# Part of the attention scores of later batches computed in early slots and kept in DRAM

## The chip, the cores and the metric

The kernel runs on one core of a Trainium2 chip. The metric is the time of one execution on the device, in microseconds (us); the median of three runs counts. Five engines work side by side: TensorE (PE in the profile, with its weight loads as PEld), VectorE (DVE), ScalarE (ACT), GpSimd (POOL) and SyncE (SP), which here mainly sends DMA transfers.

## The reference

Two blocks follow each other. The first is attention in which every query keeps only its 32 largest scores; the second sends every token to one of eight experts.

```python
# attention: batch 8, heads 8, sequence 576, head width 64
scores = scale * np.matmul(q, k.transpose(0, 1, 3, 2))
kth = np.partition(scores, -top_k, axis=-1)[..., -top_k:-top_k + 1]      # top_k = 32
scores = np.where(scores >= kth, scores, -1000000000.0)
scores = scores - np.max(scores, axis=-1, keepdims=True)
attn = np.exp(scores)
attn = attn / (np.sum(attn, axis=-1, keepdims=True) + 1e-09)
x = np.matmul(attn, v)          # then (B,H,S,D) -> (4608, 512)

# experts: 8 of them, 512 -> 1024 -> 512
logits = x @ w_gate
expert_idx = np.argmax(logits, axis=1)
...                             # gate_w: softmax value of the chosen expert
for e in range(E):              # over the rows sorted by expert
    h = np.maximum(x_sorted[lo:hi] @ w1[e], 0.0)
    y_sorted[lo:hi] = h @ w2[e]
out = gate_w[:, None] * y
```

All values are float32.

## The kernel before

The attention is cut into units of two heads (U = 4 units in each of B = 8 batches), and each unit into tiles of 128 queries. A slot of the main loop handles a pair of tiles, so there are 18 slots in a batch and 144 in all. The slots of a batch run in this order: four for the first unit, one for the remaining 64 queries of the first and second unit, four for the second unit, and the same for the third and fourth unit.

```python
def products(tiles):                              # TensorE: the scores
    ...
        ps = k.ps_s.tile([P, 2, SM], F32, name="sc")
    ...
    for half in range(2):
        for n, ps, h, rows, cols, first in todo:  # alternates between the two heads
            ...
            nc.tensor.matmul(ps[rows, j, 0:HF], n.q[d, cols], n.k[d, keys], start=True, stop=True)

def scores(got):                                  # ScalarE: PSUM to SBUF
    s = k.att.tile([P, 2, 2, HF], F32, name="s", bufs=2 if k.exact else 4)
    return s, [
        lambda m=m, ps=ps: nc.scalar.copy(s[:, m, :, :], ps[:, :, 0:HF]) for m, ps in enumerate(got)
    ]

def fold(s):                                      # VectorE: larger and smaller halves
    f.h = k.att.tile([P, 2, HF], F32, name="h", bufs=1)
    nc.vector.tensor_tensor(f.h, s[:, :, 0, :], s[:, :, 1, :], op=ALU.max)
    f.l = k.att.tile([P, 2, HF], F32, name="l")
    nc.vector.tensor_tensor(f.l, s[:, :, 0, :], s[:, :, 1, :], op=ALU.min)
```

The search for the 32nd largest score runs on VectorE (`MAX8` and `MATCH_REPLACE8`, four rounds). Then ScalarE computes `low` and a steep ramp, GpSimd subtracts it (`less`), ScalarE takes the exponential, and TensorE transposes the weights and multiplies them with the values. Small VectorE steps, such as the reciprocal of the row sums, wait in a list `aside` and are put one at a time between the instructions of a search (`tick`).

The main loop, cut to what matters here. The engines TensorE, ScalarE and VectorE get their instructions in the order of this text; SyncE and GpSimd are ordered by the scheduler of the framework.

```python
AHEAD = 3
for i, (b, g) in enumerate(work):
    ...
    if i + 1 < len(work):
        f_of[i + 1] = fold(s_of[i + 1])
        then = lambda: fold_on(f_of[i + 1])
    low, nbias, doubts = search(tiles, s_of[i], f_of.pop(i), then)
    at_place("small")
    w_of[i] = depths(s_of[i], low)                # ScalarE
    less(s_of.pop(i), w_of[i])                    # GpSimd
    ...
    if i + AHEAD < len(work):
        s_of[i + AHEAD], steps = scores(got_of.pop(i + AHEAD))
        for step in steps:
            step()
    evacuate()
    at_place("turn")
    turns = turning(i - 1) if i else iter(())
    next(turns, None)                             # transposes, copies
    part = min(BETWEEN, now - now // 2)
    rest = pieces(part)                           # pieces of expert blocks (TensorE)
    next(turns, None)
    rest = pieces(now - now // 2 - part + rest)
    weights(tiles, w_of[i], nbias)                # ScalarE: exponentials
    next(turns, None)
    evacuate()
    if i + AHEAD + 1 < len(work):
        multiply(i + AHEAD + 1)                   # products four slots ahead
    ...
```

The expert blocks (128 rows each) start in the third batch, when the rows of complete blocks are known. A block needs its rows from DRAM and the two weights of its expert, all sent by SyncE; two pairs of weight buffers exist. How many pieces a slot takes follows from a rate fixed in the program.

```python
def load_weights(n, expert):
    e = nc.sync.value_load(expert, min_val=0, max_val=E - 1)
    n.w1 = k.wp.tile([P, 1, DT, F], F32, name="w1")
    nc.sync.dma_start(n.w1, w1v[:, bass.ds(e, 1), :, :])      # 2 MiB
    n.w2 = k.wp.tile([P, 1, FT, Dm], F32, name="w2")
    nc.sync.dma_start(n.w2, w2v[:, bass.ds(e, 1), :, :])      # 2 MiB
    return n
```

Of the kernel before, what the change touches and what calls it, by code (L numbers as in the profile page):

```python
# [9 lines left out]
F32 = mybir.dt.float32  # L10
# [25 lines left out]
def kernel(  # L36
# [6 lines left out]
    moe_w2: bass.AP,  # L43
    out: bass.AP,
):

# [34 lines left out]
    nc = tc.nc  # L83
    B, U, P, _ = qk.shape
    N, Dm = out.shape
    S = N // B
    E = moe_w_gate.shape[1]
    F = moe_w1.shape[2]
    D = P // 2
    NC = 4  # L90
    SM = NC * P
    ST = S - SM
    KC = NC + 1
    HF = S // 2
# [4 lines left out]
    DT = Dm // P  # L99
    FT = F // P  # L100
# [18 lines left out]
    k = SimpleNamespace()  # L119
# [48 lines left out]
    for odd in range(2):  # L168
        for h in range(2):
            r = slice(h * D, (h + 1) * D)  # L170
            at = odd * (lw + P) + h * E
# [107 lines left out]
    def scores(got):  # L279
# [5 lines that stand above are left out]
# [445 lines left out]
    ON_CHIP = 3  # L730
    KEEP = 3 * PIECES
    BETWEEN = 2

    with fast:
        units = [(b, u) for b in range(B) for u in range(U)]
# [67 lines left out]
        def ending(b, u):  # L803

            nonlocal left
            n = unit[b * U + u]
            if u == 0:
                x_of[b] = k.xp.tile([P, KC, XW], F32, name="x")
                in_turn(token_ids(x_of[b][:, :, Dm + 1].bitcast(I32), b))
                lg_of[b] = k.small.tile([P, KC, E], F32, name="lg")  # L810
            x, lg = x_of[b], lg_of[b]
            out_steps = outputs(n, x)
            yield "products"
            next(out_steps)
            yield "relu"
            next(out_steps)
            if u % 2 == 0:
                yield "relu"
            div = divisors(n)
            next(div)  # L820
            aside.append(div)
            yield "products"
            next(out_steps)
            if b * U + u + 2 < len(units):
                load_values(unit[b * U + u + 2])
            yield "relu"
            next(out_steps)
            yield "products"
            next(out_steps)
            yield "relu"  # L830
            next(out_steps, None)
            yield "rows"
            through(div)
            logits(n, lg)
            rows(n, x)
            if u < U - 1:
                return
            yield "small"
            r = choice(lg)
            aside.append(r.steps)  # L840
            yield "weights"
            yield "turn"
            through(r.steps)
            nc.scalar.activation(lg, lg, AF.Exp)
            yield "products"
            ranks(r)
            yield "small"
            steps = places(r, x)
            aside.append(steps)
            yield "relu"  # L850
            nc.scalar.copy(run, r.run)
            yield "pool"
            through(steps)
            scatters.extend(scattering(r, x))
            if b == B - 1:
                scatter(KC)
                slot_i = k.small.tile([1, 2, NSLOT], I32, name="slot_i")
                through(table(slot_i, SURE, False))
                firsts = [(slot_i[0:1, 0, j:j + 1], slot_i[0:1, 1, j:j + 1]) for j in range(SURE)]
                ready = load_rows(SimpleNamespace(), firsts[0][1], True)  # L860
            new = LAST - SURE if b == B - 1 else new_of[b]
            if new:
                slot_i = slot_last if b == B - 1 else k.small.tile([1, 2, NSLOT], I32, name="slot_i")
                steps = table(slot_i, new, b == B - 1)
                aside.append(steps)
                yield "weights"
                yield "pool"
                yield "weights"
                yield "pool"
                through(steps)  # L870
                coming.extend((slot_i[0:1, 0, j:j + 1], slot_i[0:1, 1, j:j + 1]) for j in range(new))
            if b == B - 1:
                spare.extend(coming[ALWAYS - SURE:])
                del coming[ALWAYS - SURE:]
                assert len(loaded) == 2 and not waiting
                fill_up()
                coming[0:0] = [(firsts[0][0], ready)] + [(expert, (piece,)) for expert, piece in firsts[1:]]
                scatter(0)
# [9 lines left out]

        got_of, s_of, f_of, w_of = {}, {}, {}, {}

        def tiles_of(i):
            b, g = work[i]
            return [(unit[b * U + u], tile) for u, tile in g]
# [3 lines left out]

        def multiply(i):
            tiles = tiles_of(i)
            got_of[i] = products(tiles)  # L900
            n, tile = tiles[0]
            more = n.b * U + n.u + 2
            if tile == (NC - 1 if n.u % 2 else 2 * NC) and more < len(units):
                unit.append(load_unit(*units[more]))

        def loop():
            nonlocal credit, rate, clock
            for i in range(min(AHEAD, len(work))):
                multiply(i)
                s_of[i], steps = scores(got_of.pop(i))  # L910
                for step in steps:
                    step()
            multiply(AHEAD)
            f_of[0] = fold(s_of[0])
            fold_on(f_of[0])
            for i, (b, g) in enumerate(work):
                tiles = tiles_of(i)
                u, tile = g[0]
                if tile == 0 and u % 2 == 0:
                    open_unit(tiles[0][0])  # L920
                if tails(tiles):
                    open_unit(tiles[1][0])

                then = lambda: None
# [5 lines that stand above are left out]
                w_of[i] = depths(s_of[i], low)  # L930
                less(s_of.pop(i), w_of[i])
                doubts()
                put_stores()
                scatter(1)
                at_place("pool")
                at_place("relu")
                at_place("rows")
                at = i % per_batch
                if at == FIRST and b:
                    rate = new_of[b - 1] * PIECES / (U * NT)  # L940
                credit += rate * len(g)
                room = left
                if b == B - 1 and at >= ARRIVED:
                    room -= KEEP
                    credit = room / (len(work) - i)
                share = {0: 0.5, 1: 1.2, 2: 1.6, 3: 0.5, 2 * NC: 1.4}[tile]
                now = max(0, min(int(credit * share + 0.5), room))
                credit -= now
                clock = i
                if i + AHEAD < len(work):  # L950
                    s_of[i + AHEAD], steps = scores(got_of.pop(i + AHEAD))
                    for step in steps:
                        step()
                evacuate()
                at_place("turn")
                turns = turning(i - 1) if i else iter(())
                next(turns, None)
                part = min(BETWEEN, now - now // 2)
                rest = pieces(part)
                next(turns, None)  # L960
                rest = pieces(now - now // 2 - part + rest)
                weights(tiles, w_of[i], nbias)
# [3 lines that stand above are left out]
                    multiply(i + AHEAD + 1)  # L966
                if tile == NC - 1:
                    end = ending(b, u)
                    late.append([end, next(end)])
                at_place("products")  # L970
                at_place("weights")
                credit = min(credit + pieces(now // 2 + rest), 6 * rate)

            for _ in turning(len(work) - 1):
                pass
            assert len(late) == 1
            clock = None
            for place in late[0][0]:
                if place == "rows":
                    pieces(4)  # L980
            kept = left - ALWAYS * PIECES
            assert kept >= 0, kept
            k.apart = True
            pieces(kept)
# [135 lines left out]
```

## Time and profile before

| | |
|---|---|
| median of 3 runs | 1374.13 us (1373.11 to 1375.44) |
| span of the profiled execution | 1370.3 us |
| PE busy | 1234.6 us (90%) |
| DVE busy | 1084.5 us (79%) |
| ACT busy | 932.0 us (68%) |
| POOL busy | 661.5 us (48%) |
| DMA | 231.68 MB, mean 169 GB/s |

The shares are means over stages that differ. A view that cuts the span into stretches shows the busy time of each engine in each of them. A view of the waits says for which instruction of which engine another one stood idle, how long in total, how often, and how long at most. A tile's view lists the instructions that read or write it, with the shortest, median and longest duration in ns. A timeline lists instructions by start and duration in us; `x8` means that eight were merged. `SPq` is SyncE's queue: the time at which it sends a transfer. L290 is line 290 of the kernel.

### The profile page before, as it was taken

Reading aid. Unit: us, or ns where it says so; the run is one execution under the profiler, and the core shown is the slowest. Engines: PE = TensorE matmul, PEld = TensorE weight load, DVE = VectorE, ACT = ScalarE, POOL = GpSimd, SP = SyncE. Lnnn points to the kernel's source line nnn. Section 1 sums busy time; section 2 is a strip of 40 time slices with the busy share of each in tenths; the row PEclk is TensorE's granted clock in tenths of the full one; section 3 lists DMA queues with packets and bytes.
Section 4 is the critical chain, followed back from the end, with each engine's and each line's share of the span. In section 5 each row is a group of like instructions: output and inputs, shape, how many; then the busy total and the mean of one; then the engine's idle time right before and its main releaser. Section 6 shows DMA issues by size and latency. Waiting matters only on the chain. (4 is left out here: it accounts for less than half of the span.)

```text
span 1370.3 us, 24487 instructions
## 1 busy us (share of the span) xinstructions
PE 1234.6 (90%) x7666; PEld 838.6 (61%) x7666; DVE 1084.5 (79%) x4591; ACT 932.0 (68%) x2113; POOL 661.5 (48%) x805
## 2 busy tenths in 40 slices
PE   5777677687799999999999999999999999999995
PEld 3444444344466666766666666767676677776773
DVE  8999999999999999999999999999999820000000
ACT  4788877877888888888877788887777821111110
POOL 3455557555654666566556665565557621000000
PEclk8788787877999999999999999999999999999998
DMA  2100011001583267427654474357542859999880
GB/s 82 29 29 29 28 36 56 29 29 44 178 296 124 89 232 266 142 72 261 226 174 168 166 274 148 113 188 293 184 167 75 308 183 358 390 325 331 301 321 18
DMA packets 102220, 231.68 MB, mean 169 GB/s; under 512 B 5182, under 2 KB 25918, under 8 KB 102080
## 3 DMA queue, kind: packets, MB, share of 16 engines
q1 hardware_dynamic: 95328, 209.76, 43.8%
q0 software_dynamic: 6464, 19.97, 4.0%
q8 instruction: 62, 1.02, 0.3%
q14 instruction: 78, 0.64, 0.1%
q10 hardware_dynamic: 288, 0.30, 0.1%
HBM read 208.72 MB, written 22.33 MB: 169 GB/s over the span
## 5 line engine op out<-in xcount | busy, mean ns | idle before, releaser
L379 POOL TENSOR_TENSOR w<-s,w 128x576 f32<-128x576 f32 x288 | 409.5, 1442 | 432.3 <-ACT w L370 432.3
L687 PE MATMUL ph<-xTs,w 128*128 128x128 f32 x2560 | 308.6, 276 | 6.0 <-ACT xTs L664 6.0
L687 PEld LDWEIGHTS ph<-xTs,w 128*128 128x128 f32 x2560 | 297.4, 192 | 26.4 <-issue 19.1
L702 PE MATMUL py<-w,hT 128*128 128x512 f32 x640 | 292.2, 596 | 0.0
L338 DVE MAX8 tops<-scr 128x8 f32<-128x168 f32 x864 | 245.5, 316 | 0.0
L276 PE MATMUL sc<-qkb 64*128 64x288 f32 (+1 forms) x1280 | 221.6, 472 | 9.5 <-ACT s L283 5.2
L387 ACT ACTIVATE w<-w,nbias 128x576 f32<-128x576 f32 x288 | 224.0, 792 | 3.5 <-POOL w L379 2.5
L370 ACT ACTIVATE w<-s,low 128x576 f32<-128x576 f32 x288 | 207.6, 768 | 4.7
L398 PE MATMUL wTm<-turn,w 128*128 128x128 f32 x1152 | 171.2, 289 | 29.0 <-ACT xl L450 17.7
L398 PEld LDWEIGHTS wTm<-turn,w 128*128 128x128 f32 x1152 | 133.1, 146 | 89.6 <-issue 35.4
L999 DVE CAST any_i<-pd 1x1 int32<-1x1 f32 x1 | 0.1, 146 | 236.0 <-PE pd L997 236.0
L702 PEld LDWEIGHTS py<-w,hT 128*128 128x128 f32 x640 | 114.4, 190 | 117.6 <-issue 116.5
L345 DVE MATCH_REPLACE8 scr<-tops,scr 128x168 f32<-128x168 f32 x576 | 176.9, 311 | 0.0
L283 ACT COPY s<-sc 128x576 f32<-128x576 f32 x288 | 169.1, 641 | 10.5 <-PE sc L276 10.5
L404 ACT COPY wT<-wTm 128x512 f32<-128x512 f32 x256 | 139.1, 604 | 38.9 <-PE wTm L398 38.6
L276 PEld LDWEIGHTS sc<-qkb 64*128 64x128 f32 (+1 forms) x1280 | 118.2, 195 | 72.9 <-issue 26.6
L432 PE MATMUL po<-wT,vb 128*64 128x288 f32 x1024 | 157.8, 457 | 0.4 <-ACT wTt L419 0.4
L708 POOL DMA_INDIRECT out_dram<-y,xg x40 | 43.1, 1078 | 211.9 <-ACT y L716 199.8
L329 DVE MAX8 few<-l 128x8 f32<-128x288 f32 x288 | 127.2, 442 | 0.0
L432 PEld LDWEIGHTS po<-wT,vb 128*64 128x64 f32 x1024 | 75.3, 152 | 78.0 <-issue 29.3
L692 ACT ACTIVATE hT<-ph 128x512 f32<-128x512 f32 x80 | 48.6, 608 | 107.3 <-PE ph L687 107.3
L290 DVE TENSOR_TENSOR h<-s 128x576 f32<-128x576 f32 x144 | 117.0, 812 | 5.8 <-ACT s L283 5.8
(116 smaller groups left out, 1433.4 us busy)
## 6 DMA issues: line engine op xcount, KB each, us to landing
w<-in_moe_w_dram SPq DMA_DIRECT2D x80, 2048.0 KB, 9.6
qkb<-in_qk_dram SPq DMA_DIRECT2D x31, 608.0 KB, 4.3
xg<-x_rows SPq DMA_DIRECT2D x40, 257.0 KB, 10.0
vb<-in_v_dram SPq DMA_DIRECT2D x32, 320.0 KB, 3.2
x_rows<-blank SPq DMA_DIRECT2D x5, 257.0 KB, 14.7
x_rows<-blank POOLq DMA_DIRECT2D x4, 257.0 KB, 8.5
x_rows<-x,posi POOLq DMA_INDIRECT x40, 3.1
out_dram<-y,xg POOLq DMA_INDIRECT x40, 6.1
```

The source lines that it names most:

```text
L276: nc.tensor.matmul(ps[rows, j, 0:HF], n.q[d, cols], n.k[d, keys], start=True, stop=True)
L283: lambda m=m, ps=ps: nc.scalar.copy(s[:, m, :, :], ps[:, :, 0:HF]) for m, ps in enumerate(got)
L338: nc.vector.max(out=tops[:, m, r * 8:(r + 1) * 8], in_=src[m])
L345: nc.vector.match_replace(out=scr[:, m, :], in_to_replace=tops[:, m, r * 8:(r + 1) * 8], in_values=src[m], imm_value=NEG,)
L370: nc.scalar.activation(w[:, m, :], s[:, m, :, :].rearrange("p j k -> p (j k)"), AF.Relu, scale=-STEEP, bias=low[:, m:m + 1],)
L379: k.last_pool = in_turn(nc.gpsimd.tensor_tensor(w[:, m, :], s[:, m, :, :].rearrange("p j k -> p (j k)"), w[:, m, :], op=ALU.subtract)).ins
L387: nc.scalar.activation(w[:, m, :], w[:, m, :], AF.Exp, scale=scale, bias=nbias[:, m:m + 1], accum_out=n.z[:, c:c + 1])
L398: nc.tensor.transpose(pm[:, c * P:(c + 1) * P], w[:, m, first:first + P], ident)
L404: nc.scalar.copy(wT[:, :, m, q], pm4)
L432: nc.tensor.matmul(po[r, 0:HF], n.v[:, c, r], rhs, start=(c == 0), stop=(c == KC - 1))
L687: nc.tensor.matmul(ph[:, f, :], n.w1[:, 0, dt, fc * P:(fc + 1) * P], n.xT[:, dt, :], start=(dt == 0), stop=(dt == DT - 1),)
L702: nc.tensor.matmul(py, hT[:, f, :], n.w2[:, 0, f, :], start=(f == 0), stop=(f == FT - 1))
```

## The change

For the fifth, sixth and seventh batch, the scores of the fourth unit's eight full tiles (four slots of a batch, twelve in all) are no longer computed in those batches. Every second slot from the second on computes half of such a pair of tiles instead, copies it to the SBUF and, when both halves are there, stores it in DRAM. The space for the unit's queries and keys and for two pairs of finished scores is taken from weight buffers, which aren't used yet at that time. Where the scores are wanted, a transfer brings them from DRAM into the buffer `s`, in the place where ScalarE copied them from PSUM. It is meant to take work from TensorE and ScalarE in a stage in which both are full, and to do it in a stage in which they are not. Besides, the reciprocal of the row sums is put on the list `aside` later.

```diff
+    EARLY_FOR = (4, 5, 6)
...
             div = divisors(n)
             next(div)
-            aside.append(div)
             yield "products"
             next(out_steps)
             ...
             yield "relu"
             next(out_steps)
+            aside.append(div)
             yield "products"
...
+        early = {}
+        for i, (b, g) in enumerate(work):
+            if b in EARLY_FOR and g[0][0] == U - 1 and g[0][1] < NC:
+                early[i] = dram.tile([P, 2, 2, HF], F32, name=f"early{i}")
+
+        def earlier():
+            todo = sorted(early)
+            own = []
+            def open_own(p):
+                ...                                # room: a buffer of w1 (p even) or w2
+                nc.sync.dma_start(room[:, 0:2 * S + ST], qk[work[todo[p * NC]][0], U - 1, :, :])
+                own.append(room)
+            open_own(0)
+            for at, i in enumerate(todo):
+                if at % NC == 0:
+                    open_own(at // NC + 1)
+                ...
+                for m in range(2):
+                    ps = k.ps_s.tile([P, 2, SM], F32, name="sc")
+                    d = slice(m * D, (m + 1) * D)
+                    for j in range(2):
+                        keys = ...
+                        nc.tensor.matmul(ps[:, j, 0:HF], room[d, cols], room[d, keys], start=True, stop=True)
+                    nc.scalar.copy(put[:, m, :, :], ps[:, :, 0:HF])
+                    if m:
+                        nc.sync.dma_start(early[i], put)
+                    yield
...
         def multiply(i):
             tiles = tiles_of(i)
-            got_of[i] = products(tiles)
+            got_of[i] = None if i in early else products(tiles)
...
+        def fetch_scores(i):
+            got = got_of.pop(i)
+            if got is None:
+                s_of[i] = k.att.tile([P, 2, 2, HF], F32, name="s", bufs=4)
+                nc.sync.dma_start(s_of[i], early[i])
+                return
+            s_of[i], steps = scores(got)
+            for step in steps:
+                step()
...
                 if i + AHEAD < len(work):
-                    s_of[i + AHEAD], steps = scores(got_of.pop(i + AHEAD))
-                    for step in steps:
-                        step()
+                    fetch_scores(i + AHEAD)
                 evacuate()
                 at_place("turn")
                 turns = turning(i - 1) if i else iter(())
                 next(turns, None)
+                if i % 2:
+                    next(ahead_of, None)
                 part = min(BETWEEN, now - now // 2)
```

More of the change, by code (lines that the diff above doesn't have):

```diff
@@ L889 @@
         got_of, s_of, f_of, w_of = {}, {}, {}, {}
+        early = {}
[6 more added lines that the diff above has]
+            def open_own(p):
+                if p * NC >= len(todo):
+                    return
+                room = k.wp.tile([P, 1, DT, F], F32, name="w1") if p % 2 == 0 else k.wp.tile(
+                    [P, 1, FT, Dm], F32, name="w2")
+                room = room.rearrange("p a b c -> p (a b c)")
+                nc.sync.dma_start(room[:, 0:2 * S + ST], qk[work[todo[p * NC]][0], U - 1, :, :])
[4 more added lines that the diff above has]
+                    open_own(at // NC + 1)
+                room = own[at // NC]
+                first = 2 * S + ST + (at % 2) * 2 * S
+                put = room[:, first:first + 2 * S].rearrange("p (m j k) -> p m j k", m=2, j=2)
+                cols = slice((at % NC) * P, (at % NC + 1) * P)
+                for m in range(2):
+                    ps = k.ps_s.tile([P, 2, SM], F32, name="sc")
+                    d = slice(m * D, (m + 1) * D)
+                    for j in range(2):
+                        keys = slice(S + (0 if m else ST) + j * HF, S + (0 if m else ST) + (j + 1) * HF)
+                        nc.tensor.matmul(ps[:, j, 0:HF], room[d, cols], room[d, keys], start=True, stop=True)
[3 more added lines that the diff above has]
+                    yield
         def tiles_of(i):
@@ L904, in multiply @@
                 unit.append(load_unit(*units[more]))
+        def fetch_scores(i):
[3 more added lines that the diff above has]
+                nc.sync.dma_start(s_of[i], early[i])
+                return
+            s_of[i], steps = scores(got)
+            for step in steps:
+                step()
         def loop():
             nonlocal credit, rate, clock
+            ahead_of = earlier()
             for i in range(min(AHEAD, len(work))):
                 multiply(i)
-                s_of[i], steps = scores(got_of.pop(i))
-                for step in steps:
-                    step()
+                fetch_scores(i)
             multiply(AHEAD)
@@ L950, in loop @@
                 if i + AHEAD < len(work):
-                    s_of[i + AHEAD], steps = scores(got_of.pop(i + AHEAD))
-                    for step in steps:
-                        step()
+                    fetch_scores(i + AHEAD)
                 evacuate()
```

## The prediction

> **What bounds the kernel now.** I read first the page's slices and the busy time of each engine by batch: the five stretches are the batches that begin at 391, 525, 660, 806 and 941 us (every 18th fold on L290).
>
> ```profile
> 391.00:525.00 134.00, 130.72 (x873) 90.07 (x871) 134.00 (x575) 113.35 (x260) 79.22 (x97) 1.00 0.53 181
> 525.00:660.00 135.00, 131.40 (x877) 90.48 (x875) 133.78 (x572) 113.07 (x261) 80.93 (x95) 1.00 0.52 184
> 660.00:806.00 146.00, 144.68 (x958) 100.55 (x959) 142.63 (x572) 116.31 (x267) 89.10 (x101) 1.00 0.54 193
> 806.00:941.00 135.00, 131.38 (x877) 90.47 (x875) 133.79 (x572) 113.07 (x261) 80.96 (x95) 1.00 0.52 182
> 941.00:1079.00 138.00, 136.70 (x894) 94.58 (x894) 134.63 (x542) 109.55 (x252) 84.30 (x96) 1.00 0.52 180
> ```
>
> The columns are stretch and length, then PE, PEld, DVE, ACT and POOL busy, clock, DMA share and GB/s. VectorE is all but full until the attention ends near 1096 us, and TensorE is almost as full from 391 us on. After 1096 us only experts run, on TensorE. From one fold L290 to the next I took the length of every slot: 7.02 us where nothing disturbs, in all batches. That is VectorE's own floor. Batches 5 and 7 (counting the first as 1) average 7.49 us, batches 6 and 8 some 8.13. So at most the excess over 7.02 can be won inside the loop, and the tail after it holds a fixed number of expert blocks.
>
> Where does the excess come from? Second view, the waits of VectorE:
>
> ```profile
> DVE rz L457 <- ACT rz L455: 10.9, 7, 6.0
> DVE h L290 <- ACT s L283: 5.8, 6, 1.5
> ```
>
> (total us, times, longest.) These are small. The rest is longer instructions: the tile answer for h has
>
> ```profile
> L290 DVE TENSOR_TENSOR h<-s x144: 726/734/1812, 7.8 to 1078.8; 128x576 f32<-128x576 f32 x144
> ```
>
> that is, 726 ns at least, 734 at the median and 1812 at most. I added up what VectorE instructions take over their usual time: 5.0, 12.3, 5.0 and 12.2 us in batches 5 to 8, against 0.9 to 3.5 before. It happens where ScalarE, and so GpSimd's subtraction L379, runs late. As a measure of lateness I took how long after the last MAX8 of a search ScalarE's low (L354) starts: 0.03 us in most early slots, and from the 13th to the 18th slot of batch 5 it is 0.50, 1.34, 1.48, 4.95, 4.04 and 4.21.
>
> Third, what goes through SyncE's queue there:
>
> ```profile
> 630.52 0.35 SPq L642 DMA_DIRECT2D xg<-x_rows  x1
> 631.09 0.38 SPq L634 DMA_DIRECT2D w<-in_moe_w_dram  x1
> 631.67 0.37 SPq L636 DMA_DIRECT2D w<-in_moe_w_dram  x1
> 632.29 2.71 SPq L642 DMA_DIRECT2D xg<-x_rows  x1
> 635.24 0.80 SPq L634 DMA_DIRECT2D w<-in_moe_w_dram  x1
> 642.83 0.37 SPq L636 DMA_DIRECT2D w<-in_moe_w_dram  x1
> 643.44 3.78 SPq L642 DMA_DIRECT2D xg<-x_rows  x1
> 648.58 0.35 SPq L141 DMA_DIRECT2D qkb<-in_qk_dram  x1
> 654.08 0.38 SPq L634 DMA_DIRECT2D w<-in_moe_w_dram  x1
> ```
>
> Four weight transfers of 2 MiB each are sent within 12 us, once the rows of the batch before are scattered. The fourth is sent at 642.83 and lands 14.6 us later, at 657.4. The heads' qkb sent at 648.58 lands after
>
> ```profile
> DMA to landing us min/median/max: 11.0/11.0/11.0
> ```
>
> against a median of 4.3 on the page. The packets of these transfers follow one another in the order of sending, at some 400 GB/s. The same comes in batch 6 (fourth weight sent at 789.47, landing 803.5) and batch 7 (923.81 and 938.4).
>
> **What the Trainium skill says.** "DMA: Bandwidth & Descriptors", section "Queues, rings and completion order": SyncE owns one row of rings, and on each DMA engine the descriptors of a ring are consumed in ring order. The trace agrees: 11.0 us for qkb behind the weights. "SBUF — State Buffer", section "SBUF: two separate sides": VectorE with two SBUF inputs and GpSimd share a port pair under an exclusive lock. The 726 to 1812 ns of L290 agree, while MAX8, with one input, stays at 0.27 to 0.36 us everywhere. "TensorE: Matmul & The Clock Gate", Part 3, "The mechanism": matmuls in different row groups overlap. The trace agrees: the 8 records of one slot's scores, alternating between two heads, end in 1.24 us although one takes 402 to 403 ns.
>
> **The change part by part.** Moved: 12 groups, the 15th to 18th slots of three batches. Their products stood four slots ahead and the copies three, so batches 5 to 7 lose 1.24 us of TensorE in each of the 11th to 14th slots and two copies L283 (2 x 0.645 = 1.3 us less overlap, 1.2) of ScalarE in the 12th to 15th: some 5 us of each engine per batch. These slots are mostly at VectorE's floor already, so the gain can only be less lateness afterwards. In batch 5 it ends in the waits and long folds of the slots that follow (9.15, 9.10 and 8.78 us instead of about 7.3, by slot lengths 5.1 us in all); the same after batch 7; after batch 6 the excess that can go is about 2 us, since only the last slots of 7.9 are late.
>
> Moved as well: the reciprocal L457 comes a slot later. Its waits in the loop are 1.6, 0.2 and 0.7 us in each of batches 6 and 8. Those that lie behind no other lateness are worth about 1 us; the 6.0 us one comes after the last slot and stays.
>
> Added early: 24 half groups, one in each of the 24 odd slots up to the 48th. Both matmuls of a half use the same head, so they don't overlap: about 1.24 us at full clock, some 1.6 at the granted 0.8, and one copy of 0.645. TensorE is busy 51 of 70 us there and ScalarE 56, and TensorE's wait for wT's bank (46.1 us in 35 times between 60 and 340 us) is just where these matmuls go. Lateness of up to 1.5 us costs VectorE nothing in batch 4 (7.02 and 7.09 us at 1.35 and 1.49). I put the early cost at 2 us. The stores and rooms, 0.6 MB each, find the DMA 10% busy.
>
> Added late: 12 fetches of 590 KB on SyncE. The order of SyncE's instructions in the built program decides here. In batch 5 it is: two qkb, vb, **fetch 1, fetch 2**, xg, w1, w2, xg, w1, w2, **fetch 3**, xg, w1, **fetch 4**. In batch 6 fetch 3 stands after the fourth weight too, and fetch 4 just behind it; batch 7 is as batch 5. Fetches 1 and 2 are sent when GpSimd has freed their buffers, near 622 and 629 us, and land before VectorE folds them at 630.3 and 637.3. Fetch 3 is another matter. VectorE wants it at 644.29 (batch 5), 789.92 (6) and 925.29 (7):
>
> ```profile
> 644.29 0.74 DVE L290 TENSOR_TENSOR h<-s 128x576 f32<-128x576 f32 x1
> ```
>
> It stands behind the fourth weight, which lands at 657.4, 803.5 and 938.4, and needs about 0.59 MB / 400 GB/s = 1.5 us more. So it lands at 658.9, 805.0 and 939.9: waits of 14.6, 15.1 and 14.6 us, together 44.3. An earlier send of the fourth weight doesn't help, as the line is full from 632 us on. Fetch 4 of batches 5 and 7 follows another 2 MiB weight: 658.9 + 0.7 (xg) + 5.4 (weight) + 1.5 = 666.5, wanted at 658.9 + 7.1 = 666.0; with the landing about 1 us each, so 2.
>
> While VectorE stands still, TensorE and ScalarE catch up, so the lateness is gone whatever the moved work saves, and the same excess comes back: 5 + 2 + 5 us. Sum: 1374.1 + 44.3 + 2 - 12 - 1 + 2 = 1409.4, say 1409.
>
> **The rivals.** (1) The relief works as meant and the fetches are hidden: -12 for the late slots, -3 for reciprocals, +2 early, so about 1361. For it speaks that fetches 1 and 2 have over 5 us to spare, and that a fetch has two slots from its buffer to its fold. Against it the order in SyncE's queue and the 14.6 us landing. (2) All is off the critical path: VectorE's 7.02 us floor holds in the relieved slots, fetches are just in time, 1374. For it speaks that the relieved slots are at the floor; against it again the queue. (3) The early part costs more than I think: each odd slot loses 1 us to GpSimd's collisions, +24 alone, about 1433 with the waits. Against it stands that ScalarE waits for VectorE's tops in 32 of some 40 slots there (35.5 us).
>
> **Range and chances.** The mechanism of fetch 3 I hold for four to one. Within it the waits may be 10 to 16 us each and the catching up 8 to 20 us in all, which gives 1390 to 1420; a part of rival (2) pulls the low end to 1388. The line at +2% is 1401.6. Faster by over 2% (below 1346.6) is beyond even rival (1), so it gets only 0.02; same 0.26; slower 0.72.
>
> **What would show it.** Right: a wait of VectorE's h for a DMA of s, some 13 to 15 us long, at the 16th slot of batches 5, 6 and 7 and hardly elsewhere; after it low starts 0.03 us behind and the next slots take about 7 us; no wait of rz for ScalarE in the loop; odd early slots still near 7.02 us. Wrong: s landing within 5 us of its send before the fold (rival 1 or 2), or early slots above 7.5 us (rival 3). If weights and fetches share the line instead of following one another, the waits shrink to some 4 us and the time comes out near 1378.

## The result and the profile after

The changed kernel took 1417.53 us (median of 4 runs, 1415.62 to 1419.21), the kernel before 1374.43. The ratio is 1.0314, with a 95% interval of 1.0295 to 1.0332: 43 us slower. The span of the profiled execution is 1414.6 us, 44.3 us more than before.

Lines of the changed kernel carry higher numbers: L294 is the fold h that was L290, L461 the reciprocal that was L457, L953 the fetch of early scores. Busy time by batch, with the stretches now starting where batches 4 to 8 start in this run:

```profile
396.00:530.00 134.00, 130.68 (x871) 90.06 (x870) 134.00 (x575) 113.27 (x259) 81.43 (x97) 1.00 0.54 192
530.00:680.00 150.00, 130.72 (x852) 90.29 (x851) 133.69 (x571) 111.87 (x259) 81.54 (x97) 0.95 0.55 192
680.00:838.00 158.00, 139.35 (x919) 98.65 (x918) 138.40 (x571) 110.03 (x253) 84.19 (x98) 0.94 0.52 184
838.00:988.00 150.00, 131.17 (x853) 90.59 (x851) 134.13 (x572) 111.21 (x255) 81.66 (x97) 0.95 0.54 190
988.00:1123.00 135.00, 133.78 (x884) 93.17 (x884) 133.74 (x543) 106.49 (x243) 79.25 (x93) 1.00 0.48 171
```

VectorE (third figure after the length) works no longer than before (in batch 6 some 4 us less), but the three batches with fetches have become longer than its work: 150, 158 and 150 us with 134, 138 and 134 us busy. The waits of VectorE name what it stands for:

```profile
DVE h L294 <- DMA s<-early: 50.3, 3, 18.3
...
DVE rz L461 <- ACT rz L459: 6.0, 1, 6.0
```

Three waits for fetched scores make 50.3 us, and the reciprocal waits only once, after the loop. The timeline of VectorE shows the first of the three, in the 16th slot of batch 5:

```profile
649.03 0.55 DVE L342 MAX8 tops<-scr 128x8 f32<-128x168 f32 x2
665.76 0.76 DVE L294 TENSOR_TENSOR h<-s 128x576 f32<-128x576 f32 x1 [16.18 <-DMA s<-early]
```

And SyncE's queue shows why:

```profile
632.52 0.33 SPq L953 DMA_DIRECT2D s<-early  x1
636.94 0.35 SPq L646 DMA_DIRECT2D xg<-x_rows  x1
637.50 0.40 SPq L638 DMA_DIRECT2D w<-in_moe_w_dram  x1
638.09 0.38 SPq L640 DMA_DIRECT2D w<-in_moe_w_dram  x1
638.72 0.38 SPq L646 DMA_DIRECT2D xg<-x_rows  x1
639.33 4.04 SPq L638 DMA_DIRECT2D w<-in_moe_w_dram  x1
646.16 0.59 SPq L640 DMA_DIRECT2D w<-in_moe_w_dram  x1
646.87 7.83 SPq L953 DMA_DIRECT2D s<-early  x1
654.93 0.47 SPq L646 DMA_DIRECT2D xg<-x_rows  x1
655.70 0.95 SPq L638 DMA_DIRECT2D w<-in_moe_w_dram  x1
656.75 2.46 SPq L953 DMA_DIRECT2D s<-early  x1
```

Fetch 2, at 632.52, goes ahead of the weights. Fetch 3 is sent at 646.87, almost 3 us before VectorE wants it, yet behind four weights of 2 MiB. Tile views of one transfer each give the time from sending to landing, first for the fourth weight (sent at 646.16), then for fetch 3:

```profile
DMA to landing us min/median/max: 18.1/18.1/18.1
DMA to landing us min/median/max: 18.8/18.8/18.8
```

So the weight lands at 664.2 and the fetch right after it, at 665.7; in batches 6 and 7 fetch 3 takes 20.2 and 18.6 us. Fetch 2 took 3.9 us. Meanwhile the line is full. Busy time in the heart of each wait (DVE is the third figure after the length; the last two are the DMA share and GB/s):

```profile
650.00:665.00 15.00, 10.22 (x85) 8.08 (x84) 0.00 (x0) 5.78 (x14) 3.97 (x4) 1.00 1.04 401
808.00:824.00 16.00, 7.72 (x63) 5.58 (x61) 0.00 (x0) 3.88 (x10) 3.26 (x4) 0.84 1.04 400
958.00:973.00 15.00, 10.87 (x91) 8.73 (x90) 0.23 (x2) 6.13 (x15) 3.98 (x4) 0.98 1.04 402
```

From one search's end to the next, the whole difference can be accounted for. Up to the 15th slot of batch 5 the changed kernel is 5.2 us behind (649.58 against 644.38), and 5.0 of it is there at the 48th slot, where the early part ends. Then it waits 16.18 us. At the 15th slot of batch 6 it is 15.87 us behind, so 5.5 us came back; it waits 18.35. At the same place of batch 7 it is 32.87 us behind, so 1.35 came back; it waits 15.73. At the end of the last search it is 44.37 us behind, so 4.2 came back. That is 5.2 + 50.3 - 11.1 = 44.4 us, as the spans say.

### The profile page after: what moved, and what is told of

Read it like the earlier page. It is cut to its first block, busy times and chain, and to the rows that moved or that the text cites. A ratio compares the mean times of both kernels' runs of the same rounds, so it can differ in the third digit from the quotient of the medians.

```text
span 1414.6 us, 24552 instructions
## 1 busy us (share of the span) xinstructions
PE 1255.2 (89%) x7666; PEld 853.4 (60%) x7666; DVE 1084.8 (77%) x4591; ACT 932.2 (66%) x2113; POOL 655.1 (46%) x805
## 5 line engine op out<-in xcount | busy, mean ns | idle before, releaser
L280 PE MATMUL sc<-qkb 64*128 64x288 f32 (+1 forms) x1184 | 214.8, 469 | 9.7 <-ACT s L287 5.2
L287 ACT COPY s<-sc 128x576 f32<-128x576 f32 x264 | 154.8, 640 | 9.1 <-PE sc L280 9.1
L294 DVE TENSOR_TENSOR h<-s 128x576 f32<-128x576 f32 x144 | 115.9, 805 | 55.0 <-DMA s<-early 50.3
L436 PE MATMUL po<-wT,vb 128*64 128x288 f32 x1024 | 153.9, 448 | 0.7 <-ACT wTt L423 0.4
## 6 DMA issues: line engine op xcount, KB each, us to landing
x_rows<-blank SPq DMA_DIRECT2D x5, 257.0 KB, 14.6
```

Source lines behind the costliest of these rows:

```text
L436: nc.tensor.matmul(po[r, 0:HF], n.v[:, c, r], rhs, start=(c == 0), stop=(c == KC - 1))
```

## The experiments

Every ratio is to the kernel before, in runs on the same chip, with its 95% interval.

**Another sender (e1).** ScalarE sends the fetches, and nothing else changes.

```diff
-                nc.sync.dma_start(s_of[i], early[i])
+                nc.scalar.dma_start(s_of[i], early[i])
```

> The changed kernel, but its twelve fetches are sent by ScalarE's queue in place of SyncE's. Theory (fetch 3 is late because it stands in SyncE's queue behind the fourth weight): the three waits of VectorE's h for s, 50.3 us in the changed kernel, shrink to under 6 us together; early cost +5, late slots -11, so 1366 to 1375 us. Rival A (the line is full, any transfer in this stage takes 15 us whoever sends it): the waits stay above 30 us and the time above 1400. Rival B (the waits hid another limit, such as TensorE): waits for s go but the time stays above 1385.

Measured: 1376.59 us, ratio 1.0018 (1.0009 to 1.0027). The waits in the profile fall to a tenth:

```profile
DVE h L294 <- DMA s<-early: 5.5, 5, 3.2
```

Fetch 3 of batch 5 is sent at 642.90 in this run, behind three weights (636.32, 636.90 and 642.65) and ahead of the fourth (646.21), and costs VectorE 0.6 us. Its packets run from 646.67 to 649.69 us. A view of the DMA from 646.6 to 649.7 shows them (q10, 0.59 MB) beside those of SyncE's queue (q1); the columns are packets, MB and share of the 16 DMA engines:

```profile
q1 hardware_dynamic: 314, 0.64, 54.6%
q10 hardware_dynamic: 144, 0.59, 46.4%
```

By then SyncE's queue had moved 3.4 MB of the burst, less than its first two weights (4.2 MB), so the fetch overtook weights sent before it. The line isn't closed to a transfer of another queue while it is full: the fetch got about half of it. It also left 4 us earlier than on SyncE's queue; how the gain divides between the two was not tried. Of the 43 us, 41 are gone by the choice of the queue alone. The Trainium skill, "DMA: Bandwidth & Descriptors", section "Issuing engines are not separate DMA queues", has it that transfers of different engines interleave on the same DMA engines, and the packets agree. It also says that starting them on several engines saves only the time of sending; there the measurement differs by these 41 us, since in the changed kernel fetch 3 landed after all four weights that stood ahead of it in its queue. The time came out 1.6 us above the expected range. The profiled execution took 1369.7 us, at the low end of a spread up to 1380.9, so this profile doesn't show what the usual executions lose; that stays open.

**Only the fetches ahead of the burst (e9).** SyncE sends as in the changed kernel, but only the first two of the four groups are computed early (and a room serves two).

```diff
-            if b in EARLY_FOR and g[0][0] == U - 1 and g[0][1] < NC:
+            if b in EARLY_FOR and g[0][0] == U - 1 and g[0][1] < 2:
```

> The changed kernel, SyncE's queue as it is, but only the first two of the four early groups of each batch (15th and 16th... that is, fetches 1 and 2) are taken; the last two are computed where they were. Theory (only fetch 3, behind the fourth weight, is late): no wait of VectorE's h for s above 2 us, the 16th slots of batches 5 to 7 near 7 us; half the early cost (+2) and less than all of the relief (-3 to -8): 1368 to 1374 us. Rival (a fetch stalls VectorE whatever its place): three waits of over 10 us remain, above 1395.

Measured: 1368.56 us, ratio 0.9960 (0.9946 to 0.9974), faster than before. VectorE's waits begin with these, and none for s is among them:

```profile
DVE any_i L1051 <- PE pd L1049: 236.1, 1, 236.1
DVE rz L461 <- ACT rz L459: 6.0, 1, 6.0
DVE mx L492 <- POOL lg L472: 5.2, 1, 5.2
DVE any_p L1046 <- POOL doubt L364: 5.1, 1, 5.1
DVE h L294 <- ACT s L287: 5.1, 5, 1.6
```

Five of the six fetches have a landing in the trace; they take

```profile
DMA to landing us min/median/max: 3.8/3.9/4.2
```

Same queue, same buffers, same size: what made the wait is the place behind the weights, not the fetch.

**Other slots (e5).** SyncE's queue again, twelve groups, but of the second unit of batches 6 to 8 (and the rooms load that unit).

```diff
-    EARLY_FOR = (4, 5, 6)
+    EARLY_FOR = ((5, 1), (6, 1), (7, 1))
...
-            if b in EARLY_FOR and g[0][0] == U - 1 and g[0][1] < NC:
+            if (b, g[0][0]) in EARLY_FOR and g[0][1] < NC:
```

> The changed kernel with its fetches on SyncE's queue as they are, but the twelve early groups are those of the second unit (the 6th to 9th slots) of batches 6 to 8, where no four weights are sent at once. Theory (the burst of four weights ahead of fetch 3 makes the wait): VectorE's waits for s fall from 50.3 to under 8 us in all, early cost +5, relief -8 to -12 in the fullest slots, so 1366 to 1374 us. Rival (SyncE's queue or the DRAM itself makes every fetch late): waits above 25 us, time above 1390.

Measured: 1370.94 us, ratio 0.9976 (0.9969 to 0.9984). Two waits for s are left, 2.8 and 2.2 us; both fetches were sent 0.5 us behind one weight. One weight ahead of a fetch costs some 2.5 us here; four cost 16 to 18.

**The relief alone (e4) and which engine it helps (e10).** In e4 the early part and the fetches are left out, and the twelve slots take the scores of the slot before, so both the products and the copies are left out; the output isn't the reference's. In e10 TensorE computes the products as before, and only ScalarE's copies are left out.

```diff
                 # e4
-                s_of[i] = k.att.tile([P, 2, 2, HF], F32, name="s", bufs=4)
-                nc.sync.dma_start(s_of[i], early[i])
+                s_of[i] = s_of[i - 1]
...
-                if i % 2:
-                    next(ahead_of, None)
                 # e10, in addition
-            got_of[i] = None if i in early else products(tiles)
+            got_of[i] = products(tiles)
...
-            if got is None:
+            if i in early:
```

> The changed kernel without early part and without fetches: the twelve slots take the scores of the slot before, so the products and copies are left out and nothing is sent (the output isn't the reference's). It shows what the relief of TensorE and ScalarE is worth at most, with the reciprocal's move. Theory: lateness before the 16th slot of batches 5 to 7 is gone, 6 to 12 us faster, 1362 to 1368. Rival (VectorE's floor holds, relief is worth nothing without the standstill): 1370 to 1374.

> As the relief alone (no early part, no fetch, scores of the slot before), but TensorE computes the products of the twelve slots as before and only ScalarE's copies are left out (the output isn't the reference's). Theory (TensorE is the full engine there, 97% busy, and ScalarE is late only because it waits for TensorE): most of the 9.9 us of the relief is gone, 1369 to 1374. Rival (ScalarE's copies matter as much): 1363 to 1368.

Measured: e4 1363.93 us, ratio 0.9931 (0.9918 to 0.9945); e10 1373.90, ratio 1.0001 (0.9992 to 1.0009). The relief is worth 9.8 us, and nothing of it is left when TensorE keeps its work. ScalarE's twelve pairs of copies, 15 us of busy time, are by themselves worth nothing that can be measured. No run left out the products alone, so whether the copies add something once TensorE is relieved stays open. (Both runs go on with the same wrong scores, which may send tokens to other experts than before; the 10 us between the two runs don't depend on that.) A likely reason is that ScalarE stands waiting for TensorE in the same stretch. In e10, between 600 and 700 us:

```profile
ACT wT L408 <- PE wTm L402: 6.9, 4, 4.0
ACT xl L454 <- PE px L447: 4.3, 3, 2.6
ACT hT L696 <- PE ph L691: 3.5, 3, 1.7
```

**The early part alone (e3, e6).** In e3 the early scores are computed and stored, but the late ones are computed as before and nothing is fetched. In e6 the early matmuls use, besides, the PSUM banks of the experts, and ScalarE copies them after its exponentials, in two pieces.

```diff
                 # e3 and e6
-            got_of[i] = None if i in early else products(tiles)
+            got_of[i] = products(tiles)
                 # e6, in addition
-                    ps = k.ps_s.tile([P, 2, SM], F32, name="sc")
...
+                        ps = k.ps_m.tile([P, SM], F32, name="es", tag="m")
+                        nc.tensor.matmul(ps[:, 0:HF], room[d, cols], room[d, keys], start=True, stop=True)
+                    yield
+                    for j, ps in enumerate(two):
+                        nc.scalar.copy(put[:, m, j, :], ps[:, 0:HF])
...
                 weights(tiles, w_of[i], nbias)
                 next(turns, None)
+                if i % 2:
+                    next(ahead_of, None)
```

> The changed kernel, but the late scores are computed as before too and nothing is fetched; the early scores are still computed and stored, and not used. Theory (by the slots of the changed kernel): the early part costs some 5 us and the reciprocal gains 1 to 4, so 1375 to 1379 us. Rival (the prediction's term): early part 2 us, 1372 to 1375. Rival (the early part costs as much as the waits): above 1390.

> As the early part alone (late scores computed as before, nothing fetched), but the early matmuls use the PSUM banks that the experts don't use yet, and ScalarE copies them after its exponentials, in two pieces. Theory (the early part costs because TensorE waits for ScalarE to free the score banks, and ScalarE's copy then waits for TensorE): 1373 to 1376 us, so 0 to 2 over the kernel before. Rival (the cost is ScalarE's time itself, 0.65 to 0.8 us in odd slots): 1377 to 1380, as with the early part alone.

Measured: e3 1378.32 us, ratio 1.0031 (1.0021 to 1.0041), so 4.6 us; e6 1376.29, ratio 1.0017 (1.0010 to 1.0025), so 2.5 us. TensorE's waits in e3 between 60 and 360 us hold one that the kernel before doesn't have, and it is gone in e6:

```profile
PE sc L928 <- ACT s L287: 6.3, 6, 2.9
```

The early matmuls stand for ScalarE to free the score banks. Both theories have a part, and e6 came out just above its theory's range: with other banks and a later place of the copies together, about half of the cost seems to go, although the intervals still overlap, and 2.5 us stay. Which of these two edits does it was not tried.

**The reciprocal alone (e2).** The kernel before with `aside.append(div)` in its later place.

> The kernel before with only the later place of the reciprocal. Theory: the waits of rz for ScalarE inside the loop (4.9 us of 10.9) go, the 6.0 us one after the loop stays, and part comes back as later lateness, since TensorE is full there: 1 to 4 us faster, 1370 to 1373. Rival: the wait only moves to h, no change (1374).

Measured: 1374.19 us, ratio 1.0005 (0.9997 to 1.0013): nothing, as the rival had it, and against the theory. The waits inside the loop are gone, but

```profile
DVE h L290 <- ACT s L283: 6.6, 6, 1.6
DVE rz L457 <- ACT rz L455: 6.0, 1, 6.0
```

h now waits 6.6 us where it waited 5.8, and slots make up the rest: in batch 6 one slot is shorter (7.28 us for 8.77), and two later 9.43 stands for 8.01. A reading that fits, though no run shows it alone: TensorE was behind, and a wait of VectorE taken out ahead of TensorE's work comes back after it.

**Together (e7, e8, e11).** e7 is e1 with e6's banks. e8 is e7 with other groups, those of the second unit of batches 6 and 8 and of the fourth unit of batch 7. e11 goes back to SyncE's queue, keeps e6's banks, and takes twelve groups as in e9, the first two of a unit each, so that no fetch stands behind four weights.

```diff
                 # e11
-    EARLY_FOR = (4, 5, 6)
+    EARLY_FOR = ((4, 3), (5, 1), (5, 3), (6, 3), (7, 1), (7, 3))
...
-            if b in EARLY_FOR and g[0][0] == U - 1 and g[0][1] < NC:
+            if (b, g[0][0]) in EARLY_FOR and g[0][1] < 2:
```

> The changed kernel with fetches on ScalarE's queue and the early matmuls in the experts' PSUM banks. If early banks and queue are separate costs: the time with ScalarE's queue (1376.6) less what the other banks save (0 to 4), so 1372 to 1377 us; waits of h for s under 10 us in the profile. Rival (fetches on ScalarE's queue keep another 5 us of cost whatever the early part does, because weights and fetches share the line): not below 1375.

> Fetches on ScalarE's queue, early matmuls in the experts' PSUM banks, and groups of the second unit of batches 6 and 8 (6th to 9th slots) and of the fourth unit of batch 7. Theory: relief of -10 as with the relief alone, early +1 to +3, few waits: 1364 to 1369 us, faster than before. Rival (what relief gives in one batch is lost in the next, as TensorE's lateness is the same at the batch's end): 1372 to 1376.

> Twelve early groups again, fetched on SyncE's queue, but only fetches that stand ahead of the burst of weights: the first two groups of the fourth unit of batches 5 to 8 and of the second unit of batches 6 and 8; the early matmuls in the experts' PSUM banks. Theory (relief counts where TensorE is full, each fetch is free if no four weights stand ahead): early +2.5, relief -9 to -12, waits for s under 6 us: 1364 to 1368 us. Rival (after the first two groups nothing more can be won): not below the 1368.6 of the first two groups alone.

Measured: e7 1370.51 us, ratio 0.9976 (0.9966 to 0.9986); e8 1368.63, ratio 0.9956 (0.9943 to 0.9969); e11 1362.89, ratio 0.9923 (0.9909 to 0.9936). e7's rival falls, but e7 also lies 1.5 us below the expected range: it is 6 us faster than e1, more than the 2 us between e3 and e6; why is open. e8 is within its range. In e8 the profile has 8.2 us of waits for s in six pieces. In e11 there are

```profile
DVE h L294 <- DMA s<-early: 5.5, 2, 3.2
...
DMA to landing us min/median/max: 3.7/4.1/11.5
```

(waits of VectorE, and landing of the twelve fetches from the tile view of s). The 11.5 us are those of a fetch sent 0.5 us behind one weight. e11 is 1.1 us below its range, 11.5 us faster than the kernel before and 55 faster than the changed one, with the same number of early groups and the same queue.

## Why the prediction was right, point by point

It said 1409 us, 1388 to 1420; measured were 1417.5. The mechanism was right, and the sum was 9 us short: 6.0 us of longer waits, 3.2 of a dearer early part and 1.9 that were expected back and didn't come, less 2 for a wait that didn't occur.

- *Fetch 3 waits behind the fourth weight.* Right, and shown by e1 and e9. The sum of 44.3 us measured 50.3 (16.2, 18.3 and 15.7 for 14.6, 15.1 and 14.6); two of the three lie above the range of 10 to 16 that it gave. The prediction kept the burst where it stood. In the changed kernel its first xg is sent 1.4 us (batch 5) and 4.0 us (batch 6) after the 13th search ends, for 0.2 and 2.7 before. The traces of the experiments show why. The rows that xg reads are written by a scatter that starts at the same distance from the search's end in all of them. Where fetch 2 goes out just before it (the changed kernel, e9, e11), the first xg of batch 5 is sent 1.4 to 1.5 us after the search; where it doesn't (e1 to e4, e10), 0.2 us. In the changed kernel the scatter lands 1.2 us after the search's end, in the kernel before at the end. In batch 6 VectorE also needs 14.5 us for the two slots up to fetch 3 instead of 16.3, so it comes sooner to a transfer that doesn't.
- *Fetch 4 waits 2 us more.* Wrong: it costs VectorE at most 0.2 us. In batch 5 it lands at 672.9 us, 6.4 later than predicted, and the search before its fold ends at 672.9 too: the longer wait for fetch 3 had put the need off as well. That the two met so closely is luck.
- *The early part costs 2 us.* Too small: 5.2 us by the slots, 4.6 by e3. The time of the matmuls was right: 1.24 us in most of the 24 places. The term missed that they take the score banks and can wait for ScalarE there; e6 suggests that this is about half of the cost, and the rest is open.
- *The excess comes back: 12 us and 1 for the reciprocal.* Nearly right in sum: 11.1 (5.5, 1.35 and 4.2 for 5, 2 and 5). By e2 the reciprocal is worth nothing by itself, and by e10 neither are ScalarE's copies, which the prediction counted as a relief too. That the standstill brings the time back "whatever the moved work saves" is not shown: e4 wins 9.8 us without a standstill, and no run has the standstill without the relief.
- *Rivals.* The first, relief with hidden fetches at 1361, is what e11 comes near at 1362.9, but with other groups and other banks; its term of 12 us for the late slots measured 9.8 in e4, and its 3 for the reciprocals nothing in e2. So the idea was sound and the place of the fetches was not, while the close number is in part luck. The second (1374) falls with the waits of 50.3 us, the third (24 us for the early slots) with the 4.6 of e3. The prediction's last sentence said that a line shared by weights and fetches would give 1378 with waits of some 4 us each; e1, where two queues share it, gave 1376.6, with 5.5 us of waits in all.
- *Sums and readings.* The 1433 of the third rival counts the 2 us of the early part twice (1431). The 0.27 to 0.36 us are those of one shape of MAX8, 128x168; the shorter and longer ones take 0.20 to 0.22 and 0.43 to 0.46. None is stretched as L290 is, so the argument stands.

## What to carry to other kernels

A small transfer that a full engine waits for must be judged by what stands ahead of it in its queue, not by its own 4 us: here 8 MiB of weights made it 19 to 20. Read the order of sends in the profile before and lay the new one into it; then send it ahead of the burst or from another queue. Moving work out of a full stage needn't pay on every busy engine: 15 us of ScalarE's copies alone were worth nothing; with 15 us of TensorE's products as well, they were worth 10.

## What the runs showed of the hardware that was not expected

With the line full, some sends themselves became slow: fetch 3 occupied SyncE's queue for 7.83 us, where most sends take 0.33 to 0.40. In e1 the xg behind the fourth weight took 11.37 us to send. What holds them was not tried. Packets of two queues shared the full line about evenly, 54.6 to 46.4% in 3.1 us of e1. While VectorE stood still in batch 6, the granted TensorE clock fell to 0.84 in that stretch (0.98 and 1.00 in the other two).
